# Summing one x tile in three by an adding transfer instead of on VectorE, in an FFT and two-MoE kernel

## The chip, the cores and the metric

The kernel runs on one core of one Trainium2 chip. The time is device microseconds of that core, from the run's start to its end. A profiled execution also has a span, from its first to its last instruction. Times of runs and durations inside a trace are compared with the profiled execution's own time.

## The reference

```python
def _attn_ref(x):                      # x: 8 x 3072 x 256
    X = np.fft.fft(x, axis=1)
    X = np.fft.fft(X, axis=2)
    return X.real

def _moe_ref(x, w_in, w_out):          # w_in 256 x 2048, w_out 2048 x 256
    h = x @ w_in
    g = h - np.tanh(h)
    return g @ w_out

def _moe2_ref(x, w_in, w_out, g_ln):   # w_in 256 x 1024, w_out 1024 x 256
    h = x @ w_in
    e = np.exp(h - h.max(-1, keepdims=True))
    solu = h * (e / (e.sum(-1, keepdims=True) + 1e-09))
    mu, var = solu.mean(-1, keepdims=True), solu.var(-1, keepdims=True)
    return ((solu - mu) / np.sqrt(var + 1e-06) * g_ln) @ w_out
```

The real part of a two-dimensional FFT of each of 8 batches gives 24576 rows of 256 numbers. Each row goes through the first layer (the part of h beyond its tanh) and the second (SoLU and a layer norm).

## The kernel before

The work has two stages. In the **transform stage**, the first 197 us, each batch is transformed along its 3072 rows and written to DRAM (`z_d`). The **main stage**, the other 2,700 us, reads `z_d` back in groups of 256 row pairs and does both layers. The transform along the 256 columns is not done on x: it is multiplied into the first layer's weights, by `fold_w_in` (L345: `pw` from `wi_f` and `ftab`).

The transform stage runs 24 steps q, three for each batch: b = q // 3, j = q % 3. A tile `x{b}_{j}` is 128 partitions of 2048 numbers: eight rows r of the batch, 256 columns each. `prep(q + 2)` folds it on VectorE (DVE) before its step: `sm` (L387) is the sum of the tile's two halves, 1024 numbers per partition; `cv` (L394) and `pm` (L400, L405) are further sums and differences. `transform(q)` multiplies `pm` by the tables `tts` on TensorE (PE, L445, f32), and in a batch's last step a small term (L457, `t8s` and `hl`). A batch has eight sums, each in a bank of PSUM, and there are eight banks. So after a batch's last step (j == 2) `evict(b)` copies the sums out on ScalarE (ACT, L487 and L494), and the next batch's first matmuls need these banks.

Between the folds DVE prepares the weights of both layers, which come as 64-bit numbers and are narrowed by four operations on 1024 numbers (`narrow`: L167, L170, L173, L176), after ACT's absolute value (L329). `weave` puts them between the operations of one tile's fold in turn. The four parts of the first layer's w_in, wi0 to wi3, go from L176 straight to `fold_w_in` on PE, ahead of the steps q = 6, 9, 12 and 15. Their results `wf` are rounded by ACT (L152), the rest is taken by DVE, row 0 stored by GpSimd (POOL) to `wnu_d` (L356), and a part of `wt` set to zero by POOL (L359). wo0 and on are other weights; wi20 and wi21 are the second layer's w_in.

The order of work is the program's own: each engine runs its instructions in the order in which the program issues them. All loads of x and of the weights are issued by SyncE (SP) through `load_next` (L246), which takes the next one of a fixed list, `coming`. It is called when a buffer has been read for the last time: behind `sm` in `prep` and behind L176 in `narrowed`. All these loads share four buffers of 8 KB per partition (tag `raw`), so a load waits for the reader of the load four places before it. SP also issues the stores of `evict` and the loads of `z_d` (`load_z`, L217 and L221, at q = 13); ACT issues two of the four stores of each eviction. A transfer of SP or ACT takes one of eight completion semaphores in turn, and its issue waits until the transfer that had it before has landed.

Near the end of the stage, at q = 15 to 18, `split_z` prepares the main stage's first two groups: POOL adds and subtracts (`zc`, L233), ACT rounds (`zs`, L152), POOL takes the rest (`zs`, L155). In ACT's order the roundings of q = 16 and q = 18 stand one step ahead of evict(5), at q = 17, and just ahead of evict(6), at q = 20.

Of the kernel before, what the change touches and what calls it, by code (L numbers as in the profile page):

```python
# [10 lines left out]
F32 = mybir.dt.float32  # L11
# [3 lines left out]
ALU = mybir.AluOpType  # L15
# [6 lines left out]
P = 128  # L22
NS = 384
NSJ = NS // P
# [103 lines left out]
def fft2_moe_moe_kernel(  # L128
    ctx: ExitStack, tc: tile.TileContext, xr, x8, xn, xn8, w_in, w_out, w_in2, w_out2, g_ln, tt, t8, ft, out
):  # L130
    nc = tc.nc
    ctx.enter_context(tc.manual_schedule())

    def pool(stack, name, bufs=1, **kw):
        return stack.enter_context(tc.tile_pool(name=name, bufs=bufs, reuse_waits="tile", **kw))
# [60 lines left out]
    fold = pool(stf, "fold", side="right")  # L196
# [41 lines left out]
    coming, raws = [], {}  # L238

    def load_next(eng=nc.sync):  # L240
        if not coming:
            return
        name, parts = coming.pop(0)
        raw = raws[name] = fold.tile([P, 2048], F32, tag="raw", bufs=4, name=name)
        for o, src in parts(raw):
            eng.dma_start(out=o, in_=src)  # L246

    def x_parts(b, j):
        def parts(raw):
            src = xr[b, j * P : (j + 1) * P, :]  # L250
            if b or j:
                return [(raw, src)]

            halves = [a.rearrange("p (a r) -> p a r", a=2) for a in (raw, src)]
            return [tuple(a[:, :, h * 512 : (h + 1) * 512] for a in halves) for h in range(2)]

        return f"x{b}_{j}", parts
# [31 lines left out]
    for q in range(NQ):  # L289
        if q - 1 in w_early:  # L290
            coming += w_when[q - 1]
        coming.append(x_parts(*divmod(q, NSJ)))
        if q == 3 - 1:

            coming.append(("x8", lambda raw: [(raw[0:96], x8.rearrange("p b d -> p (b d)"))]))
        if q and q - 1 not in w_early:
            coming += w_when[q - 1]
# [15 lines left out]
    for j in range(NSJ):  # L313
        load_next()
        for k in range(3):
            table(j, k)
    load_next()
    nc.sync.dma_start(out=nraw, in_=xn.rearrange("(j p) r b -> p j r b", p=P))
    nc.sync.dma_start(out=n8, in_=xn8)
# [4 lines left out]
    def scratch(name):  # L324
        return fold.tile([P, 1024], F32, tag="s", bufs=2, name=name)

    def narrowed(name, done):
        w = fold.tile([P, 1024], F32, tag="cw", bufs=3, name=f"{name}_f")
        nc.scalar.activation(out=w, in_=word_pairs(name)[:, :, 1].bitcast(F32), func=AF.Abs)  # L329

        def steps():
            yield from narrow(w, word_pairs(name))
            raws.pop(name)
            load_next()
            done(w)

        return steps()
# [41 lines left out]

    def prep(q):  # L380
        b, j = divmod(q, NSJ)
        rv = raws.pop(f"x{b}_{j}").rearrange("p (r d) -> p r d", r=8)
        ops = (ALU.add, ALU.subtract)
        sm = scratch(f"sm{b}_{j}").rearrange("p (r d) -> p r d", r=4)
        n = 4 if q else 2
        for r in range(0, 4, n):
            nc.vector.tensor_tensor(  # L387
                out=sm[:, r : r + n], in0=rv[:, r : r + n], in1=rv[:, 4 + r : 4 + r + n], op=ALU.add
            )
        load_next()  # L390
        yield
        cv = scratch(f"cv{b}_{j}").rearrange("p (u r d) -> p u r d", u=2, r=4)
        for u in range(2):
            nc.vector.tensor_tensor(out=cv[:, u], in0=sm[:, :, :P], in1=sm[:, :, P:], op=ops[u])  # L394
        yield


        pm = pmp.tile([P, 6, 2, P], F32, tag="pm", name=f"pm{b}_{j}")
        for o, at in ((1, 0), (0, 1)):
            nc.vector.tensor_tensor(  # L400
                out=pm[:, at : at + 5 : 4], in0=cv[:, :, 0:2], in1=cv[:, :, 2:4], op=ops[1 - o]
            )
        yield
        for o in range(2):
            nc.vector.tensor_tensor(  # L405
                out=pm[:, 2 + o], in0=pm[:, 0:6:5, 0], in1=pm[:, 0:6:5, 1], op=ops[1 - o]
            )
        hl[q] = pm[:, 1:5].rearrange("p o h d -> p (o h d)")
        yield
# [135 lines left out]
    for q in range(3):  # L545
        weave(prep(q))
    weave(prep_8())
    weave(prep(3), prep_nu())
    ahead = 4

# [20 lines left out]
    for q in range(NQ):  # L571
        b, j = divmod(q, NSJ)
        ending = now[:]
        now.clear()
        works = []
        if ahead <= q + 2 < NQ:
            works.append(prep(q + 2))
        works += ready
        weave(*works)
        weave(*ending)  # L580
        ready = coming_weights(q + 1)
        if folds and j == 0:
            fold_w_in(*folds.pop())
        if q == 3:
            transform_nu()
        transform(q)
        if j == NSJ - 1 and q < NQ - 1:
            evict(b)
        if q == 13:
            for n in range(2):  # L590
                load_z(n)
        if q in (15, 16, 17, 18):
            split_z(*divmod((15, 16, 17, 18).index(q), 2))
        if q == NQ - 4:
            nc.sync.dma_start(out=wnu, in_=wnu_d.rearrange("o (m p) -> p (o m)", p=P))
            nc.sync.dma_start(
                out=nu_h, in_=nu_d[:, PAIRS : PAIRS + 1].rearrange("b o -> o b").to_broadcast([P, B])
            )
# [350 lines left out]
    for step in range(steps + 2):  # L949
        n, j = divmod(step, NM)  # L950
# [129 lines left out]
```

## Time and profile before

| | |
|---|---|
| runs | 2927.8, 2927.21, 2923.53 us; median 2927.21 |
| profiled execution | 2925.64 us |
| its span | 2923.9 us |
| mean granted clock of PE | 0.997 |
| busy: PE, DVE, POOL, ACT | 99%, 82%, 67%, 62% of the span |
| DMA in the first 210 us | 61.58 MB, mean 293 GB/s |

The span is the time inside the profile, 1.7 us less than the profiled execution's time, which is 1.6 us under the median. A row of a timeline gives the start and the length of a group of instructions on one engine, and in brackets how long the engine had been idle before it and whose end released it. A transfer's row shows its issue; "to landing" is from there to the end of the data. A granted clock of 1.00 is 2.4 GHz, 0.50 is 1.2 GHz, and values between are a mix over the stretch.

### The profile page before, as it was taken

The numbers are of one execution on the slowest core, as the hardware profiler recorded it, in microseconds if no ns is written. First come the engines' busy times: TensorE is split into PE (matmuls) and PEld (weight loads), VectorE is DVE, ScalarE is ACT, GpSimd is POOL, SyncE is SP. The second block draws the span as 40 slices with busy tenths as digits, with TensorE's granted clock in tenths as the row PEclk, the third lists the DMA queues.
The fourth block names the chain that finished last, engine by engine and source line by source line (L and its number), as shares of the span: only waits on it lengthen the run. The fifth ranks groups of instructions, "written<-read, shape, count | busy, mean of one in ns | idle before, by whom it ended". The sixth has DMA issues, their size and how long they took to land. (4 is left out here: it accounts for less than half of the span.)

```text
span 2923.9 us, 49792 instructions
## 1 busy us (share of the span) xinstructions
PE 2881.3 (99%) x16799; PEld 2482.3 (85%) x16799; DVE 2403.0 (82%) x4818; ACT 1803.9 (62%) x3287; POOL 1965.2 (67%) x2413
## 2 busy tenths in 40 slices
PE   7899999999999999999999999999999999999999
PEld 3467888888888888888888888888888888888888
DVE  7897888888888888888888888888888888888885
ACT  2345666666666666666666666666666666666665
POOL 0156767777677776777777767777677766777763
PEclk9999999999999999999999999999999999999999
DMA  8781333343334334344334433443434443443331
GB/s 306 252 298 31 88 94 94 90 94 92 87 94 98 89 89 99 88 94 93 89 95 91 96 89 90 97 91 90 94 92 92 93 92 88 95 98 89 89 91 42
DMA packets 876512, 303.75 MB, mean 104 GB/s; under 512 B 788520, under 2 KB 837688, under 8 KB 872960
## 3 DMA queue, kind: packets, MB, share of 16 engines
q1 hardware_dynamic: 873536, 293.95, 40.9%
q10 hardware_dynamic: 2304, 6.29, 0.5%
q8 instruction: 132, 2.16, 0.3%
q14 instruction: 124, 1.02, 0.1%
q0 software_dynamic: 416, 0.33, 0.0%
HBM read 162.01 MB, written 138.47 MB: 103 GB/s over the span
## 5 line engine op out<-in xcount | busy, mean ns | idle before, releaser
L155 POOL TENSOR_TENSOR gh<-g,gh 128x512 fp32r<-128x512 f32 x768 | 993.2, 1297 | 469.3 <-ACT gh L152 469.3
L773 PE MATMUL x2p<-gh,wo 128*128 128x512 f32 x4608 | 1206.5, 397 | 3.6 <-POOL gh L155 2.3
L773 PEld LDWEIGHTS x2p<-gh,wo 128*128 128x128 f32 x4608 | 825.5, 189 | 166.3 <-POOL gh L155 10.7
L749 ACT ACTIVATE t<-h 128x512 f32<-128x512 f32 x768 | 459.5, 598 | 547.8 <-DVE h L743 446.3
L720 PEld LDWEIGHTS ab<-zs,wt 128*128 128x128 f32 x4608 | 649.0, 188 | 72.5 <-DVE h L743 2.7
L720 PE MATMUL ab<-zs,wt 128*128 128x256 f32 x4608 | 668.0, 280 | 2.1 <-DVE h L743 2.1
L754 DVE TENSOR_TENSOR g<-h,t 128x512 f32<-128x512 f32 x768 | 521.8, 679 | 172.0 <-ACT t L749 168.5
L152 ACT ACTIVATE gh<-g 128x512 fp32r<-128x512 f32 x768 | 480.9, 626 | 235.5 <-DVE g L754 223.1
L896 PE MATMUL po<-wo,ut 128*128 128x256 f32 x4608 | 597.8, 278 | 4.4 <-ACT ut L152 2.6
L806 PE MATMUL ph<-wi,x2s 128*128 128x512 f32 x2304 | 597.1, 394 | 0.0
L896 PEld LDWEIGHTS po<-wo,ut 128*128 128x128 f32 x4608 | 560.7, 188 | 10.1 <-POOL ut L155 5.0
L727 DVE SCALAR_TENSOR_TENSOR asb<-nb,wnu,ab 128x256 f32<-128x256 f32 x768 | 367.1, 478 | 221.1 <-PE ab L720 219.3
L806 PEld LDWEIGHTS ph<-wi,x2s 128*128 128x128 f32 x2304 | 420.0, 188 | 84.5
L155 POOL TENSOR_TENSOR ut<-um,ut 128x512 fp32r<-128x512 f32 x372 | 480.8, 1292 | 0.8 <-issue 0.8
L743 DVE TENSOR_TENSOR h<-asb,ab 128x256 f32<-128x256 f32 x768 | 328.8, 428 | 26.5
L742 DVE TENSOR_TENSOR h<-asb,ab 128x256 f32<-128x256 f32 x768 | 329.1, 429 | 26.2
L819 ACT ACTIVATE e<-ph,st 128x1024 f32<-128x1024 f32 x192 | 214.3, 1116 | 97.9 <-DVE st L817 82.1
L817 DVE TENSOR_REDUCE st<-ph 128x1 f32<-128x1024 f32 x192 | 233.6, 1216 | 3.5 <-PE ph L806 3.5
L825 DVE SCALAR_TENSOR_TENSOR u<-ph,e 128x1024 f32<-128x1024 f32 x192 | 233.6, 1217 | 0.0
L152 ACT ACTIVATE ut<-um 128x512 fp32r<-128x512 f32 x372 | 231.1, 621 | 0.0
L856 DVE STREAM_TRANSPOSE tb<-u 128x1024 f32<-128x1024 f32 x186 | 230.0, 1236 | 0.0
L836 ACT ACTIVATE e<-u,st 128x1024 f32<-128x1024 f32 x192 | 219.5, 1143 | 0.0
(101 smaller groups left out, 1531.2 us busy)
## 6 DMA issues: line engine op xcount, KB each, us to landing
mv_d<-tb SPq DMA_DIRECT2D x186, 512.0 KB, 2.6
um<-mv_d SPq DMA_DIRECT2D x744, 128.0 KB, 3.8
out<-o SPq DMA_DIRECT2D x192, 128.0 KB, 1.7
x<-xr SPq DMA_DIRECT2D x23, 1024.0 KB, 7.6
z_d<-zt SPq DMA_DIRECT2D x16, 384.0 KB, 7.4
z_d<-zt ACTq DMA_DIRECT2D x16, 384.0 KB, 6.6
wo<-w_out SPq DMA_DIRECT2D x24, 256.0 KB, 5.5
zf<-z_d SPq DMA_DIRECT2D x48, 128.0 KB, 3.3
```

Of the source, the lines that this page charges most:

```text
L152: nc.scalar.activation(out=o, in_=i, func=AF.Copy)
L155: eng.tensor_tensor(out=o, in0=i, in1=hi.bitcast(F32), op=ALU.subtract)
L720: nc.tensor.matmul(pab[:, u], wt[c][:, hw, u, o : o + P], zs[:, hz, u], start=(i == 0), stop=(i == 2))
L727: nc.vector.scalar_tensor_tensor(out=asb, in0=zg[n][1], scalar=wnu[:, m : m + 1], in1=pab[:, 0], op0=ALU.mult, op1=ALU.add)
L742: nc.vector.tensor_tensor(out=h[:, 0], in0=asb, in1=pab[:, 1], op=ALU.add)
L743: nc.vector.tensor_tensor(out=h[:, 1], in0=asb, in1=pab[:, 1], op=ALU.subtract)
L749: nc.scalar.activation(out=t, in_=h, func=AF.Tanh)
L754: nc.vector.tensor_tensor(out=g, in0=hs.pop((n, m)).rearrange("p u n -> p (u n)"), in1=ts_.pop((n, m)).rearrange("p u n -> p (u n)"), op=A ...
L773: nc.tensor.matmul(x2p[n][mt], wo1[c][:, hw, k, mt * P : (mt + 1) * P], gh[:, hg], start=(m == 0 and i == 0), stop=(m == NM - 1 and i == 2),)
L806: nc.tensor.matmul(ph[:, fs], xs[:, hx, k, tk], wi2[:, hw, k, fs], start=(k == 0 and q == 0), stop=(k == 1 and q == 2),)
L817: nc.vector.tensor_reduce(out=st[:, 0:1], in_=ph, axis=AX.X, op=ALU.max, negate=True)
L896: nc.tensor.matmul(po[:, :D], ut[:, hu, ks], wo2[:, hw, k], start=(k == 0 and q == 0), stop=(k == NK2 - 1 and q == 2),)
```

## The change

The seven tiles x1_1 to x7_1 (j == 1, from q = 4 on) are loaded in another way. SP loads the tile's first 1024 columns into a buffer of 1024 numbers per partition (tag `xa`, two of them). POOL then issues a transfer of the other 1024 columns into the same buffer, with `accum_op=add`: it adds what it brings to what is there. `load_next` goes on to the next load of the list in the same call. `prep` takes the buffer as `sm`, without L387, and calls no `load_next` for it. The buffers of tag `raw` go from four to three, so the space stays as it was (4 x 8 KB before, 3 x 8 + 2 x 4 KB now). Lines below the first edit move down by 9 to 13: L246 becomes L254 (and L249 and L250 for the two transfers), L387 L400, L345 L354, L356 L365, L487 L500.

```diff
@@ -241,7 +241,15 @@
         if not coming:
             return
         name, parts = coming.pop(0)
-        raw = raws[name] = fold.tile([P, 2048], F32, tag="raw", bufs=4, name=name)
+        if parts is None:
+
+            b, j = (int(i) for i in name[1:].split("_"))
+            raw = raws[name] = fold.tile([P, 1024], F32, tag="xa", bufs=2, name=name)
+            src = xr[b, j * P : (j + 1) * P, :]
+            eng.dma_start(out=raw, in_=src[:, :1024])
+            nc.gpsimd.dma_start(out=raw, in_=src[:, 1024:], accum_op=ALU.add)
+            return load_next(eng)
+        raw = raws[name] = fold.tile([P, 2048], F32, tag="raw", bufs=3, name=name)
         for o, src in parts(raw):
             eng.dma_start(out=o, in_=src)
 
@@ -289,7 +297,8 @@
     for q in range(NQ):
         if q - 1 in w_early:
             coming += w_when[q - 1]
-        coming.append(x_parts(*divmod(q, NSJ)))
+        b, j = divmod(q, NSJ)
+        coming.append((f"x{b}_{j}", None) if q > 3 and j == 1 else x_parts(b, j))
         if q == 3 - 1:
 
             coming.append(("x8", lambda raw: [(raw[0:96], x8.rearrange("p b d -> p (b d)"))]))
@@ -379,16 +388,20 @@
 
     def prep(q):
         b, j = divmod(q, NSJ)
-        rv = raws.pop(f"x{b}_{j}").rearrange("p (r d) -> p r d", r=8)
+        rv = raws.pop(f"x{b}_{j}")
         ops = (ALU.add, ALU.subtract)
-        sm = scratch(f"sm{b}_{j}").rearrange("p (r d) -> p r d", r=4)
-        n = 4 if q else 2
-        for r in range(0, 4, n):
-            nc.vector.tensor_tensor(
-                out=sm[:, r : r + n], in0=rv[:, r : r + n], in1=rv[:, 4 + r : 4 + r + n], op=ALU.add
-            )
-        load_next()
-        yield
+        if rv.shape[1] == 1024:
+            sm = rv.rearrange("p (r d) -> p r d", r=4)
+        else:
+            rv = rv.rearrange("p (r d) -> p r d", r=8)
+            sm = scratch(f"sm{b}_{j}").rearrange("p (r d) -> p r d", r=4)
+            n = 4 if q else 2
+            for r in range(0, 4, n):
+                nc.vector.tensor_tensor(
+                    out=sm[:, r : r + n], in0=rv[:, r : r + n], in1=rv[:, 4 + r : 4 + r + n], op=ALU.add
+                )
+            load_next()
+            yield
         cv = scratch(f"cv{b}_{j}").rearrange("p (u r d) -> p u r d", u=2, r=4)
         for u in range(2):
             nc.vector.tensor_tensor(out=cv[:, u], in0=sm[:, :, :P], in1=sm[:, :, P:], op=ops[u])
```

On DVE, x6_1's fold woven with wi20's narrowing (`sm`, `cv`, `pm` are the fold, `wi20_f` the weight). Before:

```order
L387 TENSOR_TENSOR sm6_1_915<-x6_1_835 128x1024
L167 TENSOR_SCALAR wi20_f_900<-wi20_f_900 128x1024
L394 TENSOR_TENSOR cv6_1_920<-sm6_1_915 128x512 x2
L170 TENSOR_SCALAR wi20_f_900<-wi20_f_900 128x1024
L400 TENSOR_TENSOR pm6_1_924<-cv6_1_920 128x2x256 x2
L173 SCALAR_TENSOR_TENSOR wi20_f_900<-wi20_796,wi20_f_900 128x1024
L405 TENSOR_TENSOR pm6_1_924<-pm6_1_924 128x256 x2
L176 SCALAR_TENSOR_TENSOR wi20_f_900<-wi20_796,wi20_f_900 128x1024
```

Now:

```order
L407 TENSOR_TENSOR cv6_1_913<-x6_1_830 128x512 x2
L167 TENSOR_SCALAR wi20_f_898<-wi20_f_898 128x1024
L413 TENSOR_TENSOR pm6_1_917<-cv6_1_913 128x2x256 x2
L170 TENSOR_SCALAR wi20_f_898<-wi20_f_898 128x1024
L418 TENSOR_TENSOR pm6_1_917<-pm6_1_917 128x256 x2
L173 SCALAR_TENSOR_TENSOR wi20_f_898<-wi20_791,wi20_f_898 128x1024
L176 SCALAR_TENSOR_TENSOR wi20_f_898<-wi20_791,wi20_f_898 128x1024
```

`sm6_1` is gone, `cv6_1` reads the loaded tile itself and waits for the adding transfer, and the fold's steps stand one place earlier among the narrowing's.

On POOL, from the store of wf3's row to the last of `split_z` (`x6_1`, `x7_1` are the adding transfers; `zc`, `zs` are split_z's). Before:

```order
L356 DMA wnu_d_62<-wf3_853 16x1x32
L359 MEMSET wt3_89 1x2x512
L233 TENSOR_TENSOR zc0_0_876<-zf0_768 128x128 x2
L155 TENSOR_TENSOR zs0_773<-zc0_0_876,zs0_773 128x256
L233 TENSOR_TENSOR zc0_1_910<-zf0_768 128x128 x2
L155 TENSOR_TENSOR zs0_773<-zc0_1_910,zs0_773 128x256
L233 TENSOR_TENSOR zc1_0_974<-zf1_774 128x128 x2
L155 TENSOR_TENSOR zs1_779<-zc1_0_974,zs1_779 128x256
L233 TENSOR_TENSOR zc1_1_1014<-zf1_774 128x128 x2
L155 TENSOR_TENSOR zs1_779<-zc1_1_1014,zs1_779 128x256
```

Now:

```order
L250 DMA x6_1_830<-xr 128x1024
L365 DMA wnu_d_62<-wf3_851 16x1x32
L368 MEMSET wt3_89 1x2x512
L233 TENSOR_TENSOR zc0_0_874<-zf0_767 128x128 x2
L155 TENSOR_TENSOR zs0_772<-zc0_0_874,zs0_772 128x256
L233 TENSOR_TENSOR zc0_1_908<-zf0_767 128x128 x2
L155 TENSOR_TENSOR zs0_772<-zc0_1_908,zs0_772 128x256
L233 TENSOR_TENSOR zc1_0_968<-zf1_773 128x128 x2
L155 TENSOR_TENSOR zs1_778<-zc1_0_968,zs1_778 128x256
L250 DMA x7_1_975<-xr 128x1024
L233 TENSOR_TENSOR zc1_1_1014<-zf1_773 128x128 x2
L155 TENSOR_TENSOR zs1_778<-zc1_1_1014,zs1_778 128x256
```

The add of x6_1 stands ahead of the store, the memset and all of `split_z`, the add of x7_1 ahead of its last part. Those of x3_1, x4_1 and x5_1 stand in the same place ahead of the stores of wf0, wf1 and wf2, those of x1_1 and x2_1 ahead of the stores to `nu_d`.

On SP, the loads and stores issued at q = 13 and after, with the semaphores that an issue waits for (`DMAHW` 0 to 7 are the eight of SP's and ACT's transfers, `DMASW` those of POOL's). Before:

```order
L221 DMA nb0_771<-nu_d_66 128x256 [waits DMAHW2_49,DMASW4_49]
L217 DMA zf1_774<-z_d0_67 128x2x128 [waits DMAHW3_49]
L217 DMA zf1_774<-z_d0_67 128x2x128 [waits DMAHW4_49]
L221 DMA nb1_777<-nu_d_66 128x256 [waits DMAHW5_49]
L246 DMA x6_0_782<-xr 128x2048 [waits DMAHW6_49,DVE_49]
L246 DMA wi20_796<-w_in2 128x2048 [waits DMAHW1_49,DVE_49,Activation_49]
L488 DMA z_d4_71<-zt4_1_0_816 128x768 [waits DMAHW2_49,Activation_49]
L488 DMA z_d4_71<-zt4_1_1_820 128x768 [waits DMAHW3_49,Activation_49]
L246 DMA x6_1_835<-xr 128x2048 [waits DMAHW4_49,DVE_49]
L246 DMA wi21_883<-w_in2 128x2048 [waits DMAHW6_49,DMAHW5_49,DVE_49]
L246 DMA x6_2_897<-xr 128x2048 [waits DVE_49,Activation_49]
```

Now:

```order
L221 DMA nb0_770<-nu_d_66 128x256 [waits DMAHW5_49,DMASW6_49]
L217 DMA zf1_773<-z_d0_67 128x2x128 [waits DMAHW6_49]
L217 DMA zf1_773<-z_d0_67 128x2x128 [waits DMAHW7_49]
L221 DMA nb1_776<-nu_d_66 128x256 [waits DMAHW0_49]
L254 DMA wi20_791<-w_in2 128x2048 [waits DMAHW1_49,DVE_49]
L501 DMA z_d4_71<-zt4_1_0_811 128x768 [waits DMAHW2_49,Activation_49]
L501 DMA z_d4_71<-zt4_1_1_815 128x768 [waits DMAHW3_49,Activation_49]
L249 DMA x6_1_830<-xr 128x1024 [waits DMAHW4_49,DMASW1_49]
L254 DMA wi21_833<-w_in2 128x2048 [waits DMAHW5_49,DVE_49]
L254 DMA x6_2_881<-xr 128x2048 [waits DMAHW6_49,DVE_49,Activation_49]
L254 DMA x7_0_895<-xr 128x2048 [waits DMAHW1_49,DVE_49,Activation_49]
```

x6_0 has moved to four places above the first of these rows, ahead of all `z_d` loads, and waits for wi3's L176 instead of `sm5_1`; x6_1 is a half, waits for the buffer of x4_1's add, and stands behind nb1 and wi20, which now wait for the two semaphores (0 and 1) that ACT's stores of batch 4 hold. x7_0 waits for wi20's L176 instead of `sm6_1`.

## Rows read from the trace of the kernel before

**Rows 1.** Page, part 1: busy time, share of the span, instructions.

```profile
PE 2881.3 (99%) x16799; PEld 2482.3 (85%) x16799; DVE 2403.0 (82%) x4818; ACT 1803.9 (62%) x3287; POOL 1965.2 (67%) x2413
```

**Rows 2.** Timeline of PE, 0 to 230 us: start, length, group, [idle before <- releaser].

```profile
30.81 2.29 PE L457 MATMUL pz<-t8s,hl 96*128 96x384 f32 x6 [6.20 <-DVE hl L155]
33.03 7.57 PE L445 MATMUL pz<-tts,pm 64*128 64x384 f32 x24
...
91.09 5.37 PE L345 MATMUL pw<-wi_f,ftab 128*128 128x512 f32 x8 [3.87 <-DVE wi_f L176]
...
117.31 5.37 PE L345 MATMUL pw<-wi_f,ftab 128*128 128x512 f32 x8 [3.87 <-DVE wi_f L176]
...
141.18 3.67 PE L345 MATMUL pw<-wi_f,ftab 128*128 128x512 f32 x8 [1.52 <-DVE wi_f L176]
...
156.10 16.07 PE L445 MATMUL pz<-tts,pm 64*128 64x384 f32 x56
171.71 1.44 PE L457 MATMUL pz<-t8s,hl 96*128 96x384 f32 x6
173.08 5.74 PE L445 MATMUL pz<-tts,pm 64*128 64x384 f32 x24
179.80 10.75 PE L445 MATMUL pz<-tts,pm 128*128 128x384 f32 x32 [0.98 <-ACT zt L487]
...
191.85 5.74 PE L445 MATMUL pz<-tts,pm 64*128 64x384 f32 x24 [0.33 <-DVE pm L400]
```

**Rows 3.** Windows: engines' busy time in 10 us, PEclk, DMA share, GB/s.

```profile
30.00:40.00 10.00, 9.19 (x29) 6.01 (x30) 9.66 (x27) 3.38 (x9) 0.00 (x0) 0.66 0.83 340
```

**Rows 4.** Timeline of DVE: wi20's narrowing woven with x6_1's fold; a sum.

```profile
160.13 0.68 DVE L167 TENSOR_SCALAR wi_f<-wi_f 128x1024 f32<-128x1024 f32 x1
...
165.54 1.22 DVE L176 SCALAR_TENSOR_TENSOR wi_f<-wi,wi_f 128x1024 uint32<-128x1024 uint32 x1
166.68 1.22 DVE L387 TENSOR_TENSOR sm<-x 128x1024 f32<-128x1024 f32 x1
```

**Rows 5.** Timeline of SP: the issue of x6_1.

```profile
144.06 0.57 SPq L246 DMA_DIRECT2D x<-xr  x1
```

**Rows 6.** L246 from 144 to 145 us: x6_1 alone.

```profile
DMA to landing us min/median/max: 13.0/13.0/13.0
```

**Rows 7.** DMA issues, 0 to 210 us: count, KB each, median us to landing.

```profile
x<-xr SPq DMA_DIRECT2D x23, 1024.0 KB, 7.6
...
wi<-w_in SPq DMA_DIRECT2D x8, 512.0 KB, 5.7
...
wnu_d<-wf POOLq DMA_DIRECT2D x4, 2.0 KB, 4.7
nu_d<-nu POOLq DMA_DIRECT2D x1, 24.0 KB, 2.5
```

**Rows 8.** Timeline of POOL: wf3's store, wt3's memset, split_z.

```profile
145.78 0.49 POOL L356 DMA_DIRECT2D wnu_d<-wf  x1 [19.11 <-ACT wf L152]
147.89 0.94 POOL L359 MEMSET wt<- 1x1024 f32 x1 [1.62 <-DVE wt L155]
...
151.58 1.22 POOL L155 TENSOR_TENSOR zs<-zc,zs 128x256 fp32r<-128x256 f32 x1 [0.53 <-ACT zs L152]
152.88 1.65 POOL L233 TENSOR_TENSOR zc<-zf 128x128 f32<-128x128 f32 x2
...
164.88 11.28 POOL L155 TENSOR_TENSOR zs<-zc,zs 128x256 fp32r<-128x256 f32 x1 [6.90 <-ACT zs L152]
```

**Rows 9.** Timeline of ACT ahead of evict(6).

```profile
177.92 0.42 ACT L152 ACTIVATE zs<-zc 128x256 fp32r<-128x256 f32 x1 [13.12 <-POOL zc L233]
178.25 1.13 ACT L329 ACTIVATE wo_f<-wo 128x1024 f32<-128x1024 f32 x1
179.29 1.60 ACT L487 COPY zt<-pz 128x384 f32<-128x384 f32 x4
```

**Rows 10.** Waits of SP's queue, 0 to 200 us: us, times, longest.

```profile
SPq L246 <- DMA z_d<-zt: 3.2, 2, 2.0
```

## The prediction

> **What bounds the kernel now.** I read the page's busy shares first: PE is busy 99% of the span [rows 1], so over most of the kernel only PE's own work counts. The edit touches only the transform stage, the first 200 us. So I went on to PE's timeline for that stretch and looked only for rows with idle time before them, because these are the only places where DVE, ACT, POOL or the loads can move the end. Five such rows matter [rows 2]. Two `pw` groups wait 3.87 us each, and a third 1.52 us, for DVE's last narrowing operation (L176). The first `pz` group of batch 7 waits 0.98 us for ACT's eviction (L487). One 6.20 us wait at 30.81 us lies ahead of the first changed tile; it shows what a stall costs afterwards. The window over it has a mean granted clock of 0.66, part at 1.2 and part at 2.4 GHz [rows 3]. Behind that idle time 6 matmuls took 2.29 us where later ones take 1.44, and 24 took 7.57 where later ones take 5.74 [rows 2]: 0.85 + 1.83 = 2.7 us more. Behind each 3.87 us stall 8 matmuls took 5.37 us against 3.67 behind the 1.52 us stall: 1.7 us more. So a stall of about 4 us costs 1.7 us on top, one of 6 us 2.7 us, one of 1.5 us nothing.
>
> Then DVE's timeline, for what feeds L176: there the removed operation stands, 1.22 us [rows 4]. Then SP's issues and landings, for when x6_1 arrives, and last POOL's and ACT's timelines for the work now standing behind the adding transfers.
>
> **What it removes.** Seven L387 operations, 1.22 us each [rows 4], 8.5 us of DVE. Only those on the way to a PE wait count. x3_1, x4_1 and x5_1 are folded on DVE in front of the three L176 that PE waits for, so DVE reaches the third one 3 x 1.22 = 3.7 us earlier. PE's second stall does not shrink: PE arrives earlier too, as the first stall shrinks, and L176 still ends last. What counts is DVE's chain, **-3.7 us** when PE reaches `pw3`. The stretches at 1.2 GHz lie beside DVE's chain and are no second gain. The sums of x1_1 and x2_1 cover no PE wait after 30.81 us: nothing. The sums of x6_1 and x7_1 go too, but there PE waits only for ACT: nothing, with a bound of 0.98 us, the old wait.
>
> **What it adds.** Seven adding transfers of 512 KB on POOL's software queue. SP issues as many transfers as before, seven of them half as large, so bytes don't change. Each add waits on POOL, in program order, for its own first half. What is queued behind that wait is the question, and the order above answers it: the add of x6_1 stands in front of `wnu_d` of wf3, the memset of wt3 and everything of split_z. ACT rounds what split_z makes (zs) in front of evict(5), and PE's batch 6 needs the banks that evict(5) frees, since eight banks are one batch's sums. The add of x7_1 stands in front of the last `zc` pair, in the same way ahead of evict(6). Such a wait does pass from POOL to PE: at 177.92 us ACT had been idle 13.12 us for POOL's zc, then did zs, wo_f and the eviction [rows 9], and PE's 0.98 us at 179.80 came behind that.
>
> **When x6_1's first half lands (L).** Before, the 1 MB was issued at 144.06 [rows 5] and took 13.0 us [rows 6], so it landed at 157.1: the queue was full. The same transfers stand ahead of it now (x6_0, wi20, both z_d of batch 4), and now nb1 and wi20 also wait for ACT's z_d stores of batch 4 by the completion semaphores that these share (the lanes in the order rows; loads waiting for z_d are seen before too [rows 10]). Late bound: 157. Early bound: 3.7 us for the pipeline's lead, and half of a 1 MB load's usual 7.6 us [rows 7] less to carry, nearly 4: about 149.5. I take 156, near the late end, because the added lane waits eat the lead and leave the half megabyte behind the same queue.
>
> **From L to PE.** POOL: issuing the add, 0.6 us (POOL's issues of `wnu_d` take 0.49 [rows 8]; a larger one is taken a little longer), `wnu_d` 0.49, memset 0.94, zc pair 1.65, a gap of 0.5 for ACT's zs, rest 1.22, next zc pair 1.65 [rows 8]: L + 7.1. ACT: zs 0.42, wi_f 1.13, first bank's copy a fourth of 1.60 [rows 9]: L + 9.1. PE would want that bank when batch 5's last 24 matmuls are done: 156.10 + 5.74 = 161.84 before [rows 2], 158.2 now. So the stall is L + 9.1 - 158.2 = L - 149.1. With L = 156 it is **+6.9 us**; by the bounds 0.4 to 7.9. A stall of that size is followed by the slower stretch, **+2.7 us**. Batch 6 then runs from 165.1 for 16.98 us (161.84 to 179.80 less 0.98) plus 2.7, and ends at 184.8.
>
> **x7_1.** DVE now waits for the add of x6_1, at L + 0.6 + 5.0 = 161.6 (the 512 KB loads take 5.7 and the 2 KB software transfers 4.7 [rows 7]; I take 5.0 between them). Its fold with wi20's narrowing takes 6.6 us (160.13 to 166.76 [rows 4]): 168.2. With three buffers x7_0 waits for that L176, and lands 7.6 us later, at 175.8. x7_1's half follows behind stores that wait for this landing, at about 177.5, and takes the 7.6 us median in a full queue: 185. Then add issue 0.6, zc 1.65, zs 0.42, wo_f 1.13, first copy 0.4 [rows 8, 9]: bank free at 189.2. Stall 189.2 - 184.8 = **4.4 us**, where 0.98 stood: **+3.4**, and **+1.7** for the slower stretch behind it. x7_1's own sum lands at about 190.6, and PE needs the folded tile at about 200, so DVE's wait of some 9 us there is covered by the first step of batch 7.
>
> **Sum:** -3.7 + 6.9 + 2.7 + 3.4 + 1.7 = **+11.0 us**. The profiled execution took 2925.64 us (span 2923.9), 1.6 us under the median of the three runs, 2927.21. So 2936.6 on that execution's scale and **2938.2** on the median's. The unknown price is the adding transfer. No row shows one. Bounds: 2.6 us less than taken (the 2.5 us that a small software transfer can take), or the 13.0 us of a load in the full queue, 8 us more.
>
> The Trainium skill (DMA: Bandwidth & Descriptors, Anatomy of one DMA, SWDGE path) fits such a transfer as 2.0 us and 436 KB per us, an estimate of 3.2 us for 512 KB; the trace's 2 KB transfers alone took longer, and by the page the sum would be about 2 us less.
>
> **Rivals.**
> 1. *Hidden waits.* If x6_1's half lands by 149 and x7_1's by 179, PE waits at neither place and DVE's gain stays: -3.7, and up to -1.3 from the old 0.98 and 0.33 us waits: 2922 to 2923.5, in all faster than before. For it: the half is smaller and can be issued earlier. Against: a load that landed at 157.1 would have to be there 8 us earlier, behind the same queue. Chance 0.2; about half of it beyond -0.2%, if the loads run smoother as well.
> 2. *Wash.* L about 152, x7_1 in time: -3.7 + 2.9 + 1.7 and about 1: +2, 2929. Chance 0.15.
> 3. *The adding transfer is slow.* If it takes D longer than 5 us, x4_1 and x5_1 hold up DVE in front of L176 by most of D each, and x6_1 and x7_1 push x7_0's and x7_1's loads and pm back by another D or two. D = 3 gives about +20, D = 6 about +30 beyond before: 2947 to 2958. For it: each element is read as well as written, and DVE has little slack there. Chance 0.13.
> 4. *DVE holds POOL up at the issue.* At 164.88 one POOL operation took 11.28 us beside a busy DVE, against 1.22 for the same work [rows 8]. If that hits the adds of x4_1 and x5_1, issued amid DVE's narrowing, each may come up to 10 us late, +11 to +31: 2938 to 2958. The adds of x6_1 and x7_1 go out while DVE waits for them and would not be hit. Chance 0.07. The Trainium skill (SBUF — State Buffer, Who interferes with whom) has such a rule: a DMA issued by GpSimd can be starved of port time for its descriptors by a DVE operation in a two-port mode. No row here shows it for a descriptor.
>
> **Numbers.** Forecast 0.45, rivals 0.2, 0.15, 0.13 and 0.07. About 0.2% (5.9 us) is what a measurement can tell. Faster: half of rival 1, 0.10. Same: the other half and rival 2, 0.25. Slower: 0.65. The forecast's own range is 2933 to 2948 (L from 153 to 157, add cost up to 8 us more); the range reaches from rival 1's upper half to the slow adds: 2923 to 2958.
>
> **What would show it.** Right: no L387 for x3_1 to x7_1; the stall before `pw3` under 1 us or gone, PE there 3 to 4 us earlier; an idle of about 7 us before batch 6's first `pz`, released by ACT's zt, with POOL's zc late behind x6_1's add and PE slow behind it; about 4 before batch 7's. DVE waits of 5 to 10 us for x6_1 and x7_1. Main stage unchanged. Wrong: POOL past x6_1's add by 149 us (rival 1), PE stalls before `pw2` and `pw3` longer than before (rivals 3, 4), or a difference that grows behind 210 us, for which I have no mechanism.

## The result and the profile after

The changed kernel takes **2944.93 us** (median of 4 runs, 2943.5 to 2947.73) against 2925.82 us for the kernel before: 19.1 us slower, ratio 1.0070 with a 95% interval of 1.0058 to 1.0083. The forecast was slower by 11.0 us, 2938.2, with a range of 2923 to 2958. The sign, the range and the places were right; the size was not, and one term of the sum had the wrong sign.

The page's head (the span, then busy time, share and instructions of each engine) has DVE's seven sums less, and PE's share down by a point [rows 1]:

```profile
span 2942.6 us, 49793 instructions
...
PE 2887.2 (98%) x16799; PEld 2484.0 (84%) x16799; DVE 2391.0 (81%) x4811; ACT 1804.7 (61%) x3287; POOL 1955.4 (66%) x2420
```

PE's timeline (start, length, group, idle time before it and what ended that) shows where the time is, against [rows 2]:

```profile
90.82 6.59 PE L354 MATMUL pw<-wi_f,ftab 128*128 128x512 f32 x8 [4.21 <-DVE wi_f L176]
...
118.38 6.46 PE L354 MATMUL pw<-wi_f,ftab 128*128 128x512 f32 x8 [3.99 <-DVE wi_f L176]
...
144.31 5.37 PE L354 MATMUL pw<-wi_f,ftab 128*128 128x512 f32 x8 [2.48 <-DVE wi_f L176]
...
171.75 12.29 PE L458 MATMUL pz<-tts,pm 128*128 128x384 f32 x32 [5.10 <-ACT zt L500]
...
197.32 13.29 PE L458 MATMUL pz<-tts,pm 128*128 128x384 f32 x32 [6.62 <-ACT zt L500]
...
212.64 5.74 PE L458 MATMUL pz<-tts,pm 64*128 64x384 f32 x24 [1.05 <-DVE pm L413]
218.36 1.67 PE L733 MATMUL ab<-zs,wt 128*128 128x256 f32 x12
```

The main stage begins at 218.36 us; before, it began at 197.57. The difference of 20.8 us does not grow after that: the whole span is 18.7 us longer, and the main stage, in which nothing was changed, took 2.1 us less in this execution. The stage's waits from `pw1` on add up to 4.21 + 3.99 + 2.48 + 5.10 + 6.62 + 1.05 = 23.5 us, where they were 10.6 in [rows 2]. That is 12.9. Another 8 us is PE at the slower clock behind these waits: the three `pw` groups take 6.59, 6.46 and 5.37 us (5.37, 5.37 and 3.67 before), and the first `pz` groups of batches 6 and 7 take 12.29 and 13.29 us for 32 matmuls, 10.50 at full speed.

DVE waits for each of the last five adding transfers. On its timeline `cv` is now the first operation that reads the tile:

```profile
83.91 1.29 DVE L407 TENSOR_TENSOR cv<-x 128x512 f32<-128x512 f32 x2 [3.60 <-DMA x<-xr]
...
110.09 2.67 DVE L407 TENSOR_TENSOR cv<-x 128x512 f32<-128x512 f32 x2 [2.01 <-DMA x<-xr]
...
137.39 1.29 DVE L407 TENSOR_TENSOR cv<-x 128x512 f32<-128x512 f32 x2 [1.76 <-DMA x<-xr]
...
169.97 1.29 DVE L407 TENSOR_TENSOR cv<-x 128x512 f32<-128x512 f32 x2 [9.14 <-DMA x<-xr]
...
201.95 1.29 DVE L407 TENSOR_TENSOR cv<-x 128x512 f32<-128x512 f32 x2 [12.43 <-DMA x<-xr]
```

3.60, 2.01 and 1.76 us in front of the three narrowings that PE waits for, then 9.14 and 12.43 us for x6_1 and x7_1. On POOL's timeline (a DMA row is an issue) the add of x6_1 and all that stands behind it go out only when its first half has landed:

```profile
76.83 0.91 POOL L250 DMA_DIRECT2D x<-xr  x1 [20.30 <-DMA x<-xr]
...
162.04 0.89 POOL L250 DMA_DIRECT2D x<-xr  x1 [28.82 <-DMA x<-xr]
162.63 0.81 POOL L365 DMA_DIRECT2D wnu_d<-wf  x1
...
164.04 0.86 POOL L233 TENSOR_TENSOR zc<-zf 128x128 f32<-128x128 f32 x2
165.43 0.73 POOL L155 TENSOR_TENSOR zs<-zc,zs 128x256 fp32r<-128x256 f32 x1 [0.53 <-ACT zs L152]
...
193.66 0.88 POOL L250 DMA_DIRECT2D x<-xr  x1 [17.57 <-DMA x<-xr]
```

Before, wf3's store went out at 145.78 and the memset began at 147.89 [rows 8], with the first `zc` right behind it. Now the store stands at 162.63 and `zc` at 164.04. On ACT's timeline the rest of the way to PE:

```profile
167.14 0.42 ACT L152 ACTIVATE zs<-zc 128x256 fp32r<-128x256 f32 x1 [0.74 <-POOL zc L233]
170.20 1.14 ACT L338 ACTIVATE wi_f<-wi 128x1024 f32<-128x1024 f32 x1 [2.64 <-DMA wnu_d<-wf]
171.24 1.61 ACT L500 COPY zt<-pz 128x384 f32<-128x384 f32 x4
...
195.47 0.42 ACT L152 ACTIVATE zs<-zc 128x256 fp32r<-128x256 f32 x1 [20.18 <-POOL zc L233]
```

The transfers themselves, from the DMA issues of the first 220 us (count, KB each, median us to landing): the half loads on SP's queue (nine, with x0_0's two, which were halved before as well) and the adding ones on POOL's.

```profile
x<-xr SPq DMA_DIRECT2D x9, 512.0 KB, 9.1
...
x<-xr POOLq DMA_DIRECT2D x7, 512.0 KB, 7.1
```

The five halves of x3_1 to x7_1 alone (L249, 60 to 200 us):

```profile
DMA to landing us min/median/max: 8.0/9.5/11.6
```

For these five tiles the whole load of 1 MB took 7.1 to 13.0 us before, with a median of 9.35. So half the bytes took as long as the whole tile had, and an add of 7.1 us stands behind it.

### The profile page after: what moved, and what is told of

The parts are those of the page before. It is cut to its first block, busy times and chain, and to the rows that moved or that the text cites. A ratio compares the mean times of both kernels' runs of the same rounds, so it can differ in the third digit from the quotient of the medians.

```text
span 2942.6 us, 49793 instructions
## 1 busy us (share of the span) xinstructions
PE 2887.2 (98%) x16799; PEld 2484.0 (84%) x16799; DVE 2391.0 (81%) x4811; ACT 1804.7 (61%) x3287; POOL 1955.4 (66%) x2420
```

## The experiments

Times are medians; "before" is the kernel before, run beside each of them, 2924.6 to 2925.0 us. The theories that the expectations name: **A**, the prediction's: POOL's in-order waits for the late halves of x6_1 and x7_1, with adds that come late in front of L176. **B**: the loss of the fourth buffer makes all loads late. **C**: the adding transfer itself is slow. **D** came from the trace after: wf3's small store lands late behind x6_1's add, and ACT waits for it.

### Three buffers, no adding transfers

```diff
-        raw = raws[name] = fold.tile([P, 2048], F32, tag="raw", bufs=4, name=name)
+        raw = raws[name] = fold.tile([P, 2048], F32, tag="raw", bufs=3, name=name)
```

> The kernel before with three raw buffers instead of four, nothing else. Theory A (POOL's in-order waits for the halves of x6_1 and x7_1, and adds that land late in front of L176, cost the time): no add, no such wait, so within 4 us of before, 2922 to 2930. Theory B (the fourth buffer's loss makes the loads late, and the adds are its victims): most of the 19 us is here already, 2935 to 2945, with PE waits ahead of batches 6 and 7. Theory C (the adding transfer itself is slow): as A.

Measured: 2932.77 us against 2924.86, +7.9; ratio 1.0026 (1.0016 to 1.0035). Neither A nor B as stated: the loss of the fourth buffer costs on its own, but under half of the 19. Its PE timeline:

```profile
90.85 5.27 PE L345 MATMUL pw<-wi_f,ftab 128*128 128x512 f32 x8 [6.60 <-DVE wi_f L176]
...
118.04 5.33 PE L345 MATMUL pw<-wi_f,ftab 128*128 128x512 f32 x8 [4.94 <-DVE wi_f L176]
...
143.08 3.67 PE L345 MATMUL pw<-wi_f,ftab 128*128 128x512 f32 x8 [2.73 <-DVE wi_f L176]
...
167.96 12.87 PE L445 MATMUL pz<-tts,pm 128*128 128x384 f32 x32 [4.23 <-ACT zt L487]
```

and ACT's, where wi21's first operation (L329) stands in front of evict(5):

```profile
166.41 1.14 ACT L329 ACTIVATE wi_f<-wi 128x1024 f32<-128x1024 f32 x1 [8.13 <-DMA wi<-w_in]
```

With three buffers wi21's load was issued at 161.46 us (149.91 before) and landed at 166.30. ACT waited 8.13 us for it with the eviction queued behind, and PE 4.23 us for the bank. It is the same way into PE that the prediction described for POOL, with a load in POOL's place, and I had no rival for it.

### Four buffers and one xa buffer

```diff
-            raw = raws[name] = fold.tile([P, 1024], F32, tag="xa", bufs=2, name=name)
+            raw = raws[name] = fold.tile([P, 1024], F32, tag="xa", bufs=1, name=name)
-        raw = raws[name] = fold.tile([P, 2048], F32, tag="raw", bufs=3, name=name)
+        raw = raws[name] = fold.tile([P, 2048], F32, tag="raw", bufs=4, name=name)
```

> The changed kernel with four raw buffers and one xa buffer (the same space). A: POOL's order is the same and x6_1's half is still behind the queue, so still 8 us or more over before, 2934 to 2946. B: the loads are early again, at or under before, 2918 to 2928. C: the adds of x3_1 to x5_1 still late, 4 us or more over before, 2930 to 2940.

Measured: 2936.61 against 2924.86, +11.7; ratio 1.0037 (1.0023 to 1.0051). The time lies in the ranges of both A and C; B is out. The buffer is worth some 7 us, as without adds, and the larger part of the loss stays. PE waits 3.98, 3.99 and 3.35 us at the three `pw`, not at all ahead of batch 6, and ahead of batch 7 half as long as in the change:

```profile
187.56 13.64 PE L458 MATMUL pz<-tts,pm 128*128 128x384 f32 x32 [3.48 <-ACT zt L500]
```

The add of x6_1 was issued at 153.78 here, 8.3 us earlier than in the change.

### Copies in place of adds

```diff
-            nc.gpsimd.dma_start(out=raw, in_=src[:, 1024:], accum_op=ALU.add)
+            nc.gpsimd.dma_start(out=raw, in_=src[:, 1024:])
```

> The changed kernel with the seven adding transfers turned into plain copies of the same bytes on the same queue (the tile's second half overwrites the first, so the sum is left out). A and B: the copies land 6 to 8 us behind their issue as the adds did, and the time is that of the changed kernel, 2941 to 2948. C: they land in 3 to 5 us, DVE's waits for x3_1 to x5_1 shrink from 3.6, 2.0 and 1.8 us to under 1, and the time falls by 5 us or more, to 2932 to 2940.

Measured: 2942.51 against 2924.86, +17.7; ratio 1.0054 (1.0039 to 1.0069). The seven copies landed in a median of 5.7 us where the adds took 7.1, and their issue took POOL 0.54 to 0.62 us instead of 0.87 to 0.95:

```profile
x<-xr POOLq DMA_DIRECT2D x7, 512.0 KB, 5.7
```

DVE's waits ahead of the three narrowings went but for one of 1.0 us, and PE was at `pw3` 3.2 us earlier than with adds:

```profile
141.13 3.67 PE L354 MATMUL pw<-wi_f,ftab 128*128 128x512 f32 x8 [1.64 <-DVE wi_f L176]
```

At batches 6 and 7 it still waited 5.25 and 5.99 us. Adding instead of copying thus costs 1.4 us by the medians, 4.8 by the two profiled spans (2942.6 and 2937.8; the profiled run with copies was the shortest of its four). The time is that of A and B, the shorter waits are those of C: C is real but small.

### Only the last two, and only the first five

```diff
-        coming.append((f"x{b}_{j}", None) if q > 3 and j == 1 else x_parts(b, j))
+        coming.append((f"x{b}_{j}", None) if q > 18 and j == 1 else x_parts(b, j))
```

> The changed kernel with only x6_1 and x7_1 added by transfers; x1_1 to x5_1 are loaded whole and summed on DVE, three raw buffers as in the change. A: the two places at the end carry their 14 to 17 us, 2938 to 2944, and PE reaches pw3 as before, near 141 us. B: near the three-buffer kernel without adds, whatever that takes. C: two slow adds of seven, 2930 to 2936.

Measured: 2943.33 against 2924.86, +18.5; ratio 1.0056 (1.0041 to 1.0071). Two adding transfers of seven cost as much as all seven. That is A's time, though PE got to `pw3` at 143.26 and not near 141; ahead of batches 6 and 7 it waited 5.60 and 5.07 us.

```diff
-        coming.append((f"x{b}_{j}", None) if q > 3 and j == 1 else x_parts(b, j))
+        coming.append((f"x{b}_{j}", None) if 3 < q < 18 and j == 1 else x_parts(b, j))
```

> The changed kernel with x6_1 and x7_1 loaded whole and summed on DVE again; x1_1 to x5_1 are added by transfers, three raw buffers. If POOL's two late waits (x6_1, x7_1) carry what the change costs beyond the third buffer: the time falls to that of three buffers alone or a little under, 2929 to 2935, with POOL's first zc at about 150 us. If the adds of x3_1 to x5_1 carry it: 2937 or more.

Measured: 2935.48 against 2924.95, +10.5 (runs from 2930.39 to 2937.72); ratio 1.0032 (1.0021 to 1.0043). Between the two expectations, 2.6 us over three buffers alone; the runs of the two kernels overlap. The first five sums taken from DVE bring nothing, and most of what the adds cost beyond the buffer comes from the last two: over three buffers alone (+7.9) the first five cost 2.6 us, the last two 10.6, all seven 11.2.

### The small store moved off POOL's queue

```diff
-        nc.gpsimd.dma_start(out=wnu_d[:, c * 512 : (c + 1) * 512], in_=wf[0:1, 1])
+        nc.scalar.dma_start(out=wnu_d[:, c * 512 : (c + 1) * 512], in_=wf[0:1, 1])
```

> The changed kernel with the four small stores to wnu_d issued by ACT instead of POOL. Theory D (the store of wf3 lands late because it stands behind x6_1's add in POOL's queue, and wi21's first operation on ACT waits for it ahead of evict(5)): that wait of 2.6 us goes, PE's idle time ahead of batch 6 falls from 5.1 to some 2.5 us, and the time by 2 to 4 us, 2940 to 2943. Rival (ACT is held by the late zc anyway): PE idle 4.5 to 5.5, 2943 to 2947.

Measured: 2947.66 against 2924.95, +22.7; ratio 1.0074 (1.0058 to 1.0089). The wait of wi_f for this store went, as D has it, and PE's wait ahead of batch 6 shrank by 1.1 us. Ahead of batch 7 it grew by 1.9:

```profile
170.10 12.29 PE L458 MATMUL pz<-tts,pm 128*128 128x384 f32 x32 [4.03 <-ACT zt L500]
...
197.75 7.30 PE L458 MATMUL pz<-tts,pm 128*128 128x384 f32 x16 [8.50 <-ACT zt L500]
```

The time is over both ranges that were expected. D names a true wait, but taking it away gained nothing: x6_1's add went out at 163.70 us here, 1.7 us later than in the change.

### The adds of x6_1 and x7_1 behind split_z

```diff
-            nc.gpsimd.dma_start(out=raw, in_=src[:, 1024:], accum_op=ALU.add)
+            halves.append((raw, src))
+            if b < 6:
+                add_half()
...
+        if q in (16, 18):
+            add_half()
```

> The changed kernel with the adds of x6_1 and x7_1 moved on POOL behind split_z (x6_1's behind the second zc pair's rest, x7_1's behind the last); loads, halves and buffers as in the change. If POOL's in-order wait is the whole of the late cost: PE's idle times ahead of batches 6 and 7 (5.1 and 6.6 us, for zt) go and the time falls by 10 us or more, to 2930 to 2935. If the late halves are the cost and POOL's order only decides who waits for them: the zt waits shrink to 2 us or less, but PE waits for pm of x6_1 or x7_1 on DVE instead, some 5 to 10 us in all, and the time stays within 6 us of the change, 2939 to 2948.

Measured: 2947.22 against 2924.61, +22.6; ratio 1.0075 (1.0058 to 1.0092). This is the test of the prediction's own mechanism. POOL's `zc` began at 154.66, both waits for `zt` were gone, and the time did not fall. PE now waits for `pm` instead, in the middle of batches 6 and 7:

```profile
175.72 7.07 PE L466 MATMUL pz<-tts,pm 128*128 128x384 f32 x16 [3.36 <-DVE pm L421]
...
207.31 8.33 PE L466 MATMUL pz<-tts,pm 128*128 128x384 f32 x16 [10.97 <-DVE pm L421]
```

and DVE, ahead of these, for the same two transfers as in the change:

```profile
171.95 1.82 DVE L415 TENSOR_TENSOR cv<-x 128x512 f32<-128x512 f32 x2 [8.47 <-DMA x<-xr]
...
204.06 1.29 DVE L415 TENSOR_TENSOR cv<-x 128x512 f32<-128x512 f32 x2 [12.48 <-DMA x<-xr]
```

These two waits for `pm` come to 14.3 us, more than the 5 to 10 expected; the time stayed in the range of the second expectation. POOL's order decides who waits for x6_1 and x7_1, not whether anybody waits.

### Halves issued earlier

Three kernels issue the first half of a tile as soon as its xa buffer has been read, and not when its turn in the list of loads comes. The first keeps three `raw` and two `xa` buffers:

```diff
+    def first_half(b):
+        raw = raws[f"x{b}_1"] = fold.tile([P, 1024], F32, tag="xa", bufs=2, name=f"x{b}_1")
+        src = xr[b, P : 2 * P, :]
+        nc.sync.dma_start(out=raw, in_=src[:, :1024])
+        halves.append((raw, src))
...
+        if j == 1 and 1 <= b < B - 2:
+            first_half(b + 2)
...
+        if halves and j == ADD_AT:
+            add_half()
```

The call of `first_half` stands in `prep` behind `cv`; `ADD_AT` is 1, so `add_half` puts the add on POOL at the end of a batch's middle step.

> The changed kernel with the first halves of x3_1 to x7_1 issued as soon as their buffer has been read by cv two batches earlier, and each add put on POOL two steps later, some 25 us earlier than in the change; three raw buffers, two xa buffers. A (late halves and POOL's waits behind them): no DVE wait for an add and no late zc, so only the third buffer's cost is left, less DVE's gain: 2925 to 2932. B: the third buffer's cost as in the kernel with three buffers, 2930 to 2935. If the adds themselves disturb the other loads: 2936 or more.

Measured: 2928.27 against 2924.95, +3.3; ratio 1.0010 (1.0001 to 1.0019). Earlier halves take back 15.8 of the 19.1 us, in A's range, and DVE waits for no add any more. But PE reached `pw3` no earlier than in the change:

```profile
145.20 3.67 PE L369 MATMUL pw<-wi_f,ftab 128*128 128x512 f32 x8 [1.72 <-DVE wi_f L176]
...
201.38 1.68 PE L753 MATMUL ab<-zs,wt 128*128 128x256 f32 x12
```

With three `raw` buffers DVE now waited for tiles that are loaded whole (60 to 200 us):

```profile
DVE sm L415 <- DMA x<-xr: 5.7, 3, 3.5
```

The kernel is also 4.6 us better than three buffers without adds. That this is DVE's shorter work is not shown: the tiles x1_1 to x7_1 take no `raw` buffer here, and wi21's load, which held up the other kernel, went out at 155.03 instead of 161.46. The next one has four `raw` buffers and one `xa`, the half of batch b + 1 behind `cv` of batch b, and the add at the end of the following step (`ADD_AT` 0):

> Four raw buffers, one xa buffer, the first half of the next such tile issued behind cv of the one before, its add on POOL at the end of the next step. If late halves with POOL's waits and the third buffer are all that the change costs, DVE's gain is left: at or under before, 2919 to 2925, PE at pw3 2 to 4 us earlier than before, no wait for zt at batch 6. If adding transfers cost something that an early issue does not hide (slow adds, queueing of other loads): 2929 or more.

Measured: 2927.34 against 2924.95, +2.4; ratio 1.0010 (1.0001 to 1.0018). It falls between the two expectations, and PE was at `pw3` 2.2 us later than before, not earlier. The next kernel shows that it is the place of the add: x3_1's half had landed at 61.78, but its add went out at 76.06 and landed at 85.53; DVE waited 6.4 us in all for the adds of x3_1 to x5_1, and PE 3.46 us at `pw3`. The last one moves each add one step forward (`ADD_AT` 2), into the step of its half. POOL's order of work is then that of the change, row for row:

> As the last one (four raw buffers, one xa buffer, halves issued early), but each add put on POOL one step earlier, in the step in which its half is issued: POOL's order is then the change's own, x6_1's add ahead of wf3's store and split_z, x7_1's ahead of the last zc pair. If only late halves and the third buffer cost: the adds land 5 us or more before cv reads them, DVE's wait of 14 us for them goes, PE reaches pw3 2 to 4 us earlier than before, and the time is 2919 to 2924, under before, though POOL's order is that of the change. If the order itself costs, or halves and adds hold up the other loads: zc late or DVE waiting for sm, 2927 or more.

Measured: **2921.15 against 2924.61**, 3.5 us under before; ratio 0.9989 (0.9980 to 0.9998). It beats the change by far and the kernel before by little: the interval ends just under 1. On POOL x6_1's add still stands ahead of wf3's store and the first `zc`, but its half is there in time. ACT still waited 3.67 us for wf3's store behind it; no wait of PE came of that:

```profile
145.87 0.89 POOL L266 DMA_DIRECT2D x<-xr  x1 [20.12 <-DMA x<-xr]
146.46 0.80 POOL L380 DMA_DIRECT2D wnu_d<-wf  x1
...
147.88 1.31 POOL L233 TENSOR_TENSOR zc<-zf 128x128 f32<-128x128 f32 x2
```

DVE's waits from 60 to 200 us (in total, times, longest) have none for an added tile left:

```profile
DVE wt L155 <- ACT wt L152: 11.7, 4, 7.0
...
DVE sm L415 <- DMA x<-xr: 0.9, 1, 0.9
```

and on PE both waits for `zt` are gone:

```profile
92.80 5.44 PE L369 MATMUL pw<-wi_f,ftab 128*128 128x512 f32 x8 [6.40 <-DVE wi_f L176]
...
118.09 3.67 PE L369 MATMUL pw<-wi_f,ftab 128*128 128x512 f32 x8 [2.87 <-DVE wi_f L176]
...
140.22 3.67 PE L369 MATMUL pw<-wi_f,ftab 128*128 128x512 f32 x8 [1.48 <-DVE wi_f L176]
...
195.04 1.66 PE L753 MATMUL ab<-zs,wt 128*128 128x256 f32 x12
```

At `pw3` PE is 0.96 us ahead of the kernel before (140.22 against 141.18), not the 2 to 4 expected. From `pw1` to `pw3` it took 47.42 us where it took 50.09 before, 2.67 less, about the two sums of x4_1 and x5_1 (2.44). A longer wait at `pw1`, 6.40 for 3.87 us, takes that back. It does not come from an add: ACT's second store of batch 1 shares its completion semaphore with x3_0's load and waited for it till 71.1 us, with wf0's rounding queued behind.

### The four together

The times against before, from these runs. The early column differs from the late one in where the adds stand, too, and in its two rows they stand in different steps:

| | halves late, as in the change | halves early |
|---|---|---|
| three `raw`, two `xa` | +19.1 | +3.3 |
| four `raw`, one `xa` | +11.7 | -3.5 |

Late halves cost 15.8 and 15.2 us, the missing buffer 7.4 and 6.8 (7.9 without any add). So the change's 19.1 is about 8 for the buffer and 15.5 for the late halves, less the 4 or so by which an early kernel beats its like without adds.

Where in the stage this lies, by the start of `pw0` (the first of the four `pw` groups), of `pw3` and of the main stage on PE, in one profiled execution each:

| kernel | `pw0` | `pw3` | main stage | `pw0` to `pw3` | `pw3` to main stage |
|---|---|---|---|---|---|
| before | 66.65 | 141.18 | 197.57 | 74.53 | 56.39 |
| three `raw`, no adds | 63.67 | 143.08 | 205.67 | 79.41 | 62.59 |
| the change | 66.04 | 144.31 | 218.36 | 78.27 | 74.05 |
| the same, halves early | 67.03 | 145.20 | 201.38 | 78.17 | 56.18 |
| four `raw`, one `xa`, halves late | 67.23 | 143.59 | 208.57 | 76.36 | 64.98 |
| the same, halves early | 65.82 | 140.22 | 195.04 | 74.40 | 54.82 |

Early halves save 0.1 and 2.0 us up to `pw3`, and 17.9 and 10.2 behind it. What late halves cost is thus nearly all paid behind `pw3`, where x6_1 and x7_1 are read.

## Why the prediction was right, and where it was not

**What it removes: wrong.** The term "-3.7 us when PE reaches `pw3`" failed; PE got there 3.1 us late (144.31 against 141.18), and batch 5 began 4.8 us late behind a slower `pw3` group. That is 8.5 us of the 9.8 between the forecast and the 20.8 by which the main stage came late. I gave x3_1 to x5_1 no price for arriving late. Before, these loads landed at 72.8, 101.7 and 128.3 us, and DVE read the tiles 8.0, 5.3 and 4.9 us later:

```profile
80.82 1.22 DVE L387 TENSOR_TENSOR sm<-x 128x1024 f32<-128x1024 f32 x1
...
107.04 1.23 DVE L387 TENSOR_TENSOR sm<-x 128x1024 f32<-128x1024 f32 x1
...
133.26 1.22 DVE L387 TENSOR_TENSOR sm<-x 128x1024 f32<-128x1024 f32 x1
```

A second transfer of 7 us behind the first eats all of that. In the change DVE's three waits, 7.4 us, less the three sums, 3.7, make up the 3.7 us by which it takes longer from `pw0` to `pw3`. The leads of 8.0, 5.3 and 4.9 us could have been read in the trace before; I read only x6_1's landing. The -3.7 was seen whole at `pw3` in no run: the best early kernel gained 0.96 us there. With three `raw` buffers timely halves or shorter transfers did not bring it either: PE was at `pw3` at 145.20 with early halves, behind whole tiles that came late, and at 141.13 with copies. Rival 3 had the place (x4_1 and x5_1 in front of L176, chance 0.13) and its sign, longer stalls before `pw2` and `pw3`, was seen (3.99 for 3.87, 2.48 for 1.52). But it looked for the delay in the add alone, and the first half is the longer of the two (9.5 and 7.1 us); with copies in place of adds the time was still +17.7.

**The missing buffer: not priced.** I spoke of three buffers only where a load of x7 waits for another release. Alone they cost 7.9 us; in the profiled execution 4.9 between `pw0` and `pw3` and 6.2 behind it, there through wi21's load and ACT, less 3.0 gained ahead of `pw0`.

**x6_1: right in kind, and its size near by luck.** Forecast: half landed at 156, at the latest 157; a stall of 6.9 and 2.7 at the slower clock. Measured: half landed at 161.5, a stall of 5.10 and 1.8 (12.29 against 10.50). The half landed 5.5 us late, but PE came for the bank 8.5 us late (166.65 for 158.2), and the two errors cancel for the larger part. SP issued the half only here, 8.2 us later than the whole tile before [rows 5]:

```profile
152.30 0.54 SPq L249 DMA_DIRECT2D x<-xr  x1
```

3.1 us of that is the delay at `pw3`. The rest is SP's order: x6_0's load, now ahead of the `z_d` loads, waited for wi3's L176 till 144.2, and a load of `z_d` waited 2.0 us for x6_0's completion semaphore. The semaphores of ACT's stores, which I had named, held up nothing; these stores had landed by 145.2. POOL's part was shorter than the rows said: a `zc` pair took 0.86 us and a rest 0.73, where [rows 8] have 1.65 and 1.22. DVE stood idle at the time. The Trainium skill (SBUF — State Buffer, Who interferes with whom) states that a DVE operation with two SBUF inputs contends with GpSimd's reads; the trace agrees, with these numbers. In place of that time stood the wait for wf3's store, whose buffer wi21's first operation takes over.

**x7_1: right, too small.** Stall 6.62 for 4.4, slower stretch 2.8 for 1.7. All the late terms together: forecast 14.7, measured 16.0 (20.8 less 4.8).

**The price of an add.** Taken 5.0; median 7.1, from 6.2 to 8.5, within the bounds. The estimate of 3.2 us from the Trainium skill (DMA: Bandwidth & Descriptors, Anatomy of one DMA) was met by no transfer of this size on that queue; the shortest copy took 4.0.

**Rival 1** named the right condition, halves there in time; in the change itself it failed by 12 and 14 us. Its price, -3.7 to -5.0, is near what the last kernel gave (-3.5), but not for its reason: of the 2.5 us by which that kernel's main stage began earlier, 0.96 was there at `pw3`, and 1.3 are the old waits of 0.98 and 0.33 us. **Rival 4** did not happen: adds issued amid DVE's narrowing (x4_1 6.3, x5_1 6.2 us) landed sooner than x6_1's and x7_1's (7.9 and 8.3), issued with DVE idle.

**The deeper reason was incomplete.** I put the loss at batches 6 and 7 on POOL's order. That was the way it took, but the kernel with the adds behind split_z is no faster, and the one with the change's order and early halves is faster than before. The cause is that one load became two in series, with the first still issued at the old place in the list; the clean pair for it is that of four `raw` buffers and one `xa`, late and early, with POOL's order the same in both.

What stays open: what DVE's shorter work is worth by itself. No kernel here takes the sums from DVE without also freeing `raw` buffers or moving loads. How the cost divides is known in part: nearly all of what early halves give back lies behind `pw3`, and over three buffers alone the last two adds cost 10.6 us and the first five 2.6.

## What to carry to other kernels

Before splitting a load into two transfers that depend on each other, put its landing beside its first use for every instance: a lead of 5 to 8 us was used up by a second transfer of 7, and the two tiles that had led by 1.9 and 0.2 us before (x6_1 landed at 157.10 and was read at 158.99, x7_1 179.94 and 180.17) stopped the pipeline. If a transfer gets longer, its issue has to move forward with it; here that, with the adds moved to match, turned +19.1 into +3.3 in the same buffers. A buffer given up to pay for an idea has a price of its own, to be measured alone.

## What the runs showed of the hardware that I had not expected

A wait's length does not tell what PE's clock does behind it. In the change the 2.48 us wait before `pw3` is followed by 5.37 us for eight matmuls; in the fastest kernel a wait of 2.87 us before `pw2` is followed by 3.67. The windows over the two groups (PE, PEld, DVE, ACT and POOL busy with their counts, then PEclk, DMA share, GB/s) show a granted clock of 0.68, partly at 1.2 GHz, and one of 1.00, 2.4 GHz:

```profile
144.30:149.70 5.40, 5.39 (x9) 2.38 (x10) 4.35 (x7) 0.00 (x0) 0.00 (x0) 0.68 0.84 264
```

```profile
118.00:121.80 3.80, 3.71 (x9) 1.82 (x10) 3.70 (x6) 0.60 (x2) 0.00 (x0) 1.00 0.95 137
```

A stall priced by the wait alone was too cheap here by 8 of 21 us.

A software-queue transfer of 2 KB behind one of 512 KB landed with it: wf3's store took 7.5 us in the change (issued at 162.63, landed at 170.12, x6_1's add at 169.95). The stores of wf0 to wf2, too, landed 0.2 us behind the adds ahead of them.
